# Attention and two MoE layers on one core: the first MoE's Strassen operands formed from PSUM during attention, and its second phase taken by weight tile with both token halves

## The chip, the cores and the metric

One core of one Trainium2 chip runs the whole program. The metric is the device time of one execution, in microseconds (us). TensorE is written PE, VectorE DVE, ScalarE ACT, GpSimd POOL; SP is the engine that issues the DMAs here. PE's granted clock is given as a share of its upper level: 1.00 is 2.4 GHz, 0.50 is 1.2 GHz.

## What is computed

```python
attn = attention(q, k, v)                    # 4 batches, 8 heads, 576 positions, window 128
x = attn.transpose(0, 2, 1, 3).reshape(2304, 512)
h = x @ w_in                                 # first MoE: 512 -> 2048
r = np.maximum(h, 0.0)
x = (r * r) @ w_out                          # 2048 -> 512
...
for e in range(8):                           # second MoE: gates P by Sinkhorn, then the experts
    out += P[:, e:e + 1] * (np.maximum(x @ w1[e], 0.0) @ w2[e])
```

## The kernel before

Every matrix product is done in three passes over operands that are cut into a high part (fp32r) and the rest: high by high, high by low, low by high (`mm3`, lines 126 to 128). A *split* is the making of such a pair: ACT copies the high part, then DVE or POOL subtracts it (`split_sb` from SBUF, lines 117 and 118; `split_ps` from PSUM, lines 121 and 122).

The 2304 tokens of the first MoE are five chunks: 256, then four of 512. Chunks 0 to 2 go through a plain loop over 16 blocks f of 128 hidden columns (`gemm1`, square of the ReLU on ACT line 914 and DVE line 917, `moe1_tail` two blocks later). The steps of attention are woven into that loop, and a scheduler orders the engines' queues there. PE's product `h` of a block has one PSUM bank, which comes free when DVE has read it at line 917.

Chunks 3 and 4 (the token halves, t = 0 and 1) go together through one level of Strassen with seven products. Attention leaves their raw tokens in `xr[0]` and `xr[1]` (ACT copy, line 436). After the last attention step, in the last four blocks of chunk 2 (`early_super`), seven token operands are formed: b11, b21 and b22 are quarters of the tokens, t1 to t4 are sums and differences of quarters (DVE, lines 810 to 816), and each of the seven is split. The sums of the weights (`super_sums`, lines 839 to 843) and their splits stand in the same queues. From there on the order is as written. The **super stage** then runs eight units u of seven products p each (`s_product`, `s_evict`); its results g, two blocks f by two token halves h per unit, go to DRAM (`d_g`).

The **second phase** multiplies g by `w_out`: 32 products j of 12 matmuls each, for the first half f = 0 to 15 and then for the second half f = 0 to 15 again. Every j loads its own weight tile w (512 KB) and its g tile (256 KB) by `b_load`, five products ahead and the first four during the last unit of the super stage; `b_split` cuts g two products ahead, with the subtraction on POOL. Beside it stand the preparations for the second MoE: `load_q` (tokens back from DRAM), `x_op` (its seven token operands, alternately on DVE and POOL), `sums_w1` and `split_w1`, and `keep`, which adds the two parts of a finished chunk on POOL and stores it.

Of the kernel before, what the change touches and what calls it, by code (L numbers as in the profile page):

```python
# [29 lines left out]
def attention_moe_moe2(  # L30
# [393 lines left out]

    def put_x(ps, hp, t0, n):
        o = 0
        while o < n:
# [186 lines left out]
    def keep(c, d):  # L614
        c0, n = chunk(c)
        if True:
            if c < NCH - 1:
# [183 lines left out]
    xr_stack = ExitStack()  # L801
    sps = ExitStack()
    sx, sr, ss, sslab = {}, {}, {}, {}
    NU = NF1 // 2

    def super_x(nm, eng):

        q = {(h, t): xr[t][:, 2 * h : 2 * h + 2] for h in range(2) for t in range(2)}
        if nm == "t1":
            nc.vector.tensor_sub(q[0, 0], q[0, 1], q[0, 0])  # L810
        elif nm == "t2":
            nc.vector.tensor_sub(q[0, 0], q[1, 1], q[0, 0])
        elif nm == "t3":
            nc.vector.tensor_sub(q[0, 1], q[1, 1], q[0, 1])
        elif nm == "t4":
            nc.vector.tensor_sub(q[1, 0], q[1, 0], q[0, 0])
        at = {"b11": (0, 0), "t1": (0, 0), "t2": (0, 0), "b21": (1, 0), "t4": (1, 0), "t3": (0, 1), "b22": (1, 1)}[nm]
        x = sx[nm] = sp.tile([P, 2, 2, CH], F32R, name=f"s{nm}")
        split_sb(q[at], x[:, 0], x[:, 1], (nc.vector, nc.gpsimd)[eng])
# [37 lines left out]
    def early_super(at):  # L857
        nonlocal sp
        if at == 0:
# [5 lines left out]
            super_x("b11", 0)  # L865
            super_x("b21", 1)
        elif at == 1:
            super_sums(0, False)
            super_sums(0, True)
            super_split(0, False)  # L870
            super_x("t1", 0)
        elif at == 2:
            super_split(0, True)
            super_x("t2", 0)
            super_x("t3", 1)
        else:
            super_raw(2)
            super_x("t4", 0)
            super_x("b22", 1)

    sp = None
    for c in range(PLAIN_CH):
        c0, n = chunk(c)
        if c == 1:
# [6 lines left out]
            xp2 = xr_stack.enter_context(tc.tile_pool(name="xp2", bufs=1))  # L891
            for i in range(PLAIN_CH, NCH):
                xr.append(xp2.tile([P, NK, CH], F32, name=f"xr{i}"))

# [47 lines left out]
    xr_stack.close()  # L942
    gp = m1.enter_context(tc.tile_pool(name="gp", bufs=1))
# [11 lines left out]
    def s_product(u, p):  # L955
# [3 lines left out]
        for k in range(2):  # L959
            mm3(ps, (w[:, k, 0], w[:, k, 1]), (x[:, 0, k], x[:, 1, k]), first and k == 0, k == 1, skip_group_check=True)  # L960
# [37 lines left out]
    btiles = {}  # L998
    bparts = {}

    def b_load(j):

        if j < 2 * NF1:
            h, f = divmod(j, NF1)
            w = mp.tile([P, 2, DM], F32R, name="w", tag=("b", "a")[j % 2], bufs=(4, 3)[j % 2])
            nc.sync.dma_start(raw(w), d_out[f])
            g = gp.tile([P, CH], F32, name="gq", tag="gq", bufs=6)
            nc.sync.dma_start(g, d_g[f // 2][:, f % 2, h])
            btiles[j] = w, g

    def b_split(j):

        if j < 2 * NF1:
            g = btiles[j][1]
            hl = [rp.tile([P, CH], F32R, name=nm, tag=tag, bufs=3) for nm, tag in (("gh", "rh"), ("gl", "rl"))]
            split_sb(g, *hl)
            bparts[j] = hl

    baccs = []

    def b_product(j, ds):
        h, f = divmod(j, NF1)
        (w, _), (gh, gl) = btiles[j], bparts[j]
# [9 lines left out]
    def finish_part(c, d, acc1):  # L1033
        split_ps(acc1, xh[c][:, d], xl[c][:, d])
        if c < NCH - 1:
# [8 lines left out]
    for u, p in slots:  # L1044
        if u == NU:
            b_product(0, (0, 1))
            b_load(4)
# [7 lines left out]
        if u < 3 and p in (2, 4, 6) and keeps and u:  # L1055
            keep(*keeps.pop(0))
# [13 lines left out]
    X_AT = {4: ("b11", 0), 5: ("b21", 1), 6: ("t1", 0), 7: ("t2", 1), 8: ("t3", 0), 9: ("t4", 1), 10: ("b22", 0)}  # L1070
# [591 lines left out]
```

## Time and profile before

| | us |
|---|---|
| median of 3 runs | 2074.07 (2073.59 to 2077.26) |
| the profiled execution, its own time | 2077.16 |
| its span, first to last instruction | 2075.5 |
| PE busy | 2022.5 (97% of the span) |
| DVE, ACT, POOL busy | 1430.1, 985.9, 1127.0 |
| early stage (from the last attention step to the end of chunk 2) | about 380 to 413 |
| super stage | about 413 to 506 |
| second phase | about 506 to 602 |

A timeline row gives start, length, engine, line, operation, tiles, and in brackets how long the engine stood idle before it and who released it. A row of waits gives who waited for whom, us in total, how many times, and the longest. A row of a group gives the count, then busy us and mean ns of one, then the idle time before it. PE's matmuls overlap: a record lasts longer than the distance to the next one.

### The profile page before, as it was taken

The numbers are of one execution on the slowest core, as the hardware profiler recorded it, in microseconds if no ns is written. First come the engines' busy times: TensorE is split into PE (matmuls) and PEld (weight loads), VectorE is DVE, ScalarE is ACT, GpSimd is POOL, SyncE is SP. The second block draws the span as 40 slices with busy tenths as digits, with TensorE's granted clock in tenths as the row PEclk, the third lists the DMA queues.
The fourth block names the chain that finished last, engine by engine and source line by source line (L and its number), as shares of the span: only waits on it lengthen the run. The fifth ranks groups of instructions, "written<-read, shape, count | busy, mean of one in ns | idle before, by whom it ended". The sixth has DMA issues, their size and how long they took to land.

```text
span 2075.5 us, 31718 instructions
## 1 busy us (share of the span) xinstructions
PE 2022.5 (97%) x10821; PEld 1844.5 (89%) x10821; DVE 1430.1 (69%) x2513; ACT 985.9 (48%) x1997; POOL 1127.0 (54%) x855
## 2 busy tenths in 40 slices
PE   7989999899999999999999999999999999999999
PEld 5767777677778899999998999999999999999999
DVE  7986766664336878777776667766776677677765
ACT  7666665354344554444444444444444443444443
POOL 4224344543678788878875445544554454455442
PEclk9999999999999999999999999999999999999999
DMA  7867777346968778888789877777786777777773
GB/s 212 276 205 245 225 223 200 112 148 214 324 236 294 291 293 315 325 306 317 290 301 351 273 260 254 257 260 257 245 285 221 263 259 257 254 257 241 266 259 109
DMA packets 298721, 528.08 MB, mean 254 GB/s; under 512 B 91312, under 2 KB 138048, under 8 KB 294464
## 3 DMA queue, kind: packets, MB, share of 16 engines
q1 hardware_dynamic: 298560, 526.04, 75.4%
q8 instruction: 87, 1.43, 0.3%
q14 instruction: 74, 0.61, 0.1%
HBM read 364.92 MB, written 161.03 MB: 253 GB/s over the span
## 4 chain that ended last, share of the span: by engine, by line
PE 80%; DVE 6%; DMA 3%; ACT 2%; POOL 2%; issue 2%; SPq 0%; ACTq 0%; POOLq 0%; DVEq 0%
PE y L127 11%; PE y L128 11%; PE y L126 11%; PE g L126 10%; PE g L128 10%; PE g L127 10%; PE acc L127 1%; PE acc L128 1%; PE s L126 1%; PE s L127 1%; PE s L128 1%; PE acc L126 1%; PE h L126 1%; PE h L128 1%; PE h L127 1%
## 5 line engine op out<-in xcount | busy, mean ns | idle before, releaser
L1470 POOL TENSOR_TENSOR rb<-R,rb 128x768 fp32r<-128x768 f32 x95 | 213.9, 2252 | 345.8 <-ACT rb L1465 317.4
L1506 DVE TENSOR_TENSOR a<-y,a 128x384 f32<-128x384 f32 x420 | 232.6, 554 | 193.1 <-PE y L128 192.7
L1470 POOL TENSOR_TENSOR rt<-R,rt 128x768 fp32r<-128x768 f32 x121 | 230.3, 1915 | 138.9 <-ACT rt L1465 60.0
L118 POOL TENSOR_TENSOR w2a<-r,w2a 128x1024 fp32r<-128x1024 f32 x64 | 154.0, 2407 | 67.3 <-ACT w2a L117 67.3
L126 PE MATMUL g<-xt,w1o 128*128 128x384 f32 x512 | 173.7, 339 | 2.3 <-ACT u L1184 1.0
L128 PE MATMUL g<-xt,w1o 128*128 128x384 f32 x512 | 172.6, 337 | 0.0
L127 PE MATMUL g<-xt,w1o 128*128 128x384 f32 x512 | 172.3, 337 | 0.0
L126 PE MATMUL y<-rt,w2o 128*128 128x384 f32 x496 | 168.1, 339 | 0.0
L127 PE MATMUL y<-rt,w2o 128*128 128x384 f32 x496 | 167.9, 339 | 0.0
L128 PE MATMUL y<-rt,w2o 128*128 128x384 f32 x496 | 167.4, 337 | 0.0
L1465 ACT ACTIVATE rt<-R 128x768 fp32r<-128x768 f32 x122 | 102.7, 842 | 134.9 <-DVE R L1451 84.1
L128 PE MATMUL y<-w2a,rl 128*128 128x512 f32 x384 | 150.1, 391 | 0.0
L127 PE MATMUL y<-w2a,rh 128*128 128x512 f32 x384 | 149.6, 390 | 0.2 <-POOL w2a L118 0.2
L126 PE MATMUL y<-w2a,rh 128*128 128x512 f32 x384 | 149.5, 389 | 0.0
L1446 DVE TENSOR_TENSOR R<-R,pb 128x768 f32<-128x768 f32 x128 | 138.4, 1082 | 5.5 <-ACT R L1572 3.9
L126 PE MATMUL y<-rb,w2o 128*128 128x384 f32 x408 | 138.3, 339 | 0.6 <-DVE a L1506 0.6
L127 PE MATMUL y<-rb,w2o 128*128 128x384 f32 x408 | 138.2, 339 | 0.0
L128 PE MATMUL y<-rb,w2o 128*128 128x384 f32 x408 | 137.6, 337 | 0.0
L126 PE MATMUL g<-xb,w1o 128*128 128x384 f32 x384 | 129.9, 338 | 0.0
L128 PE MATMUL g<-xb,w1o 128*128 128x384 f32 x384 | 129.5, 337 | 0.0
L127 PE MATMUL g<-xb,w1o 128*128 128x384 f32 x384 | 129.2, 337 | 0.0
L1572 ACT ACTIVATE R<-u 128x384 f32<-128x384 f32 x128 | 67.3, 526 | 127.6 <-DVE u L1192 86.4
(316 smaller groups left out, 5896.7 us busy)
## 6 DMA issues: line engine op xcount, KB each, us to landing
w1o<-d_w SPq DMA_DIRECT2D x448, 256.0 KB, 3.1
w2o<-d_w SPq DMA_DIRECT2D x218, 512.0 KB, 4.0
d_w<-w1a SPq DMA_DIRECT2D x32, 1792.0 KB, 11.5
d_w<-w2a SPq DMA_DIRECT2D x30, 1536.0 KB, 7.8
r<-in_moe_w_dram SPq DMA_DIRECT2D x64, 512.0 KB, 4.2
w<-d_out SPq DMA_DIRECT2D x32, 512.0 KB, 5.7
u<-in_moe_w_in_dram SPq DMA_DIRECT2D x16, 512.0 KB, 5.0
u<-in_moe_w_out_dram SPq DMA_DIRECT2D x16, 512.0 KB, 5.5
```

Of the source, the lines that this page charges most:

```text
L118: (eng or nc.gpsimd).tensor_sub(lo, src, raw(hi))
L126: nc.tensor.matmul(ps, lhsT=lh, rhs=rh, start=first, stop=False, **kw)
L127: nc.tensor.matmul(ps, lhsT=lh, rhs=rl, start=False, stop=False, **kw)
L128: nc.tensor.matmul(ps, lhsT=ll, rhs=rh, start=False, stop=last, **kw)
L1446: nc.vector.tensor_mul(r, r, pb[:, None, :].to_broadcast([P, 2, HALF]))
L1465: nc.scalar.activation(x[:, 0], R[m, f, h], AF.Copy)
L1470: eng.tensor_sub(x[:, 1], R[m, f, h], raw(x[:, 0]))
L1506: nc.vector.tensor_add(acc[dst][:, dt], ps[:, :HALF], acc[dst][:, dt])
L1572: nc.scalar.activation(R[m, f, h][:, pair], src, AF.Relu)
```

## The change

Three things are changed. **(1) Token operands.** As each piece of attention output for chunks 3 and 4 leaves PSUM, `put_super` forms operands from it at once. Pieces of the first half are split straight into b11 or b21, and copied to `xr[0]` as well. Pieces of the second half: for hp 0 and 1 (quarter b12) copied, and t1 = ps - b11 formed; for hp 2 and 3 (quarter b22) split, and t2 = ps - t1, t3 = ps - b12 (DVE) and t4 = b21 - t2 (POOL) formed. In `early_super` the splits of t1 to t4 remain, all on DVE. b11 and b21 have tiles of their own; b22, t1 and t2 lie in chunk 0's and chunk 1's token tiles, which are free by then. **(2) The second phase** goes by f with both halves in turn (`border`), so that each of the 16 weight tiles is loaded once; only the last two f are done half after half. All eight PSUM banks accumulate at once. **(3) Order of the preparations.** `b_load(0)` to `b_load(4)` stand in unit 6 instead of units 7 and 8, `b_split`'s subtraction and all of `x_op` go to DVE, chunk 2's `keep`s leave the super stage for j = 14 to 17, chunk 3's come at j = 29, its gate sums at j = 30, and g lands in the space of `xr`.

```diff
+    def put_super(ps, half, hp, at, w):
+        kh, k = divmod(hp, 2)
+        (r0, r1), ts = [[xr[t][:, x] for x in (k, 2 + k)] for t in range(2)], slice(at, at + w)
+        (b11, b21), (b12, b22) = r0, r1
+        if half == 0:
+            split_ps(ps, *[x[:, k, ts] for x in sx["b21" if kh else "b11"]])
+            nc.scalar.copy(r0[kh][:, ts], ps)
+        elif kh == 0:
+            nc.scalar.copy(b12[:, ts], ps)
+            nc.vector.tensor_sub(b11[:, ts], ps, b11[:, ts])
+        else:
+            split_ps(ps, *[x[:, k, ts] for x in sx["b22"]])
+            nc.vector.tensor_sub(b22[:, ts], ps, b11[:, ts])
+            nc.vector.tensor_sub(b12[:, ts], ps, b12[:, ts])
+            nc.gpsimd.tensor_sub(b21[:, ts], b21[:, ts], b22[:, ts])
...
-                nc.scalar.copy(xr[c - PLAIN_CH][:, hp, at : at + w], ps[:, o : o + w])
+                put_super(ps[:, o : o + w], c - PLAIN_CH, hp, at, w)
...
+    def super_x(nm):
+        if nm not in sx:
+            x = sp.tile([P, 2, 2, CH], F32R, name=f"s{nm}")
+            sx[nm] = x[:, 0], x[:, 1]
+        r = {"t1": xr[0][:, :2], "t4": xr[0][:, 2:], "t3": xr[1][:, :2], "t2": xr[1][:, 2:]}[nm]
+        split_sb(r, *sx[nm], nc.vector)
...
             super_raw(1)
-            super_x("b11", 0)
-            super_x("b21", 1)
+            super_x("t2")
+            super_sums(0, False)
         elif at == 1:
-            super_sums(0, False)
+            super_split(0, False)
             super_sums(0, True)
-            super_split(0, False)
-            super_x("t1", 0)
+            super_x("t1")
         elif at == 2:
             super_split(0, True)
-            super_x("t2", 0)
-            super_x("t3", 1)
+            super_x("t3")
         else:
             super_raw(2)
-            super_x("t4", 0)
-            super_x("b22", 1)
+            super_x("t4")
...
+    border = [(0, 0), (1, 0), (0, 1), (1, 1)] + [(f, h) for f in range(2, NF1 - 2) for h in range(2)]
+    border += [(f, h) for h in range(2) for f in (NF1 - 2, NF1 - 1)]
...
-        if j < 2 * NF1:
-            h, f = divmod(j, NF1)
-            w = mp.tile([P, 2, DM], F32R, name="w", tag=("b", "a")[j % 2], bufs=(4, 3)[j % 2])
-            nc.sync.dma_start(raw(w), d_out[f])
-            g = gp.tile([P, CH], F32, name="gq", tag="gq", bufs=6)
+        if j < len(border):
+            f, h = border[j]
+            if h == 0:
+                bw[f] = mp.tile([P, 2, DM], F32R, name="w", tag="ba"[f % 2], bufs=(4, 3)[f % 2])
+                nc.sync.dma_start(raw(bw[f]), d_out[f])
+            g = bg[j] = xr[j // NK % 2][:, j % NK]
             nc.sync.dma_start(g, d_g[f // 2][:, f % 2, h])
...
-            split_sb(g, *hl)
+            split_sb(bg.pop(j), *bparts[j], nc.vector)
...
-        if u < 3 and p in (2, 4, 6) and keeps and u:
-            keep(*keeps.pop(0))
...
-        elif u == NU - 1 and p < 4:
+        elif u == NU - 2 and p < 5:
             b_load(p)
-            if p > 1:
-                b_split(p - 2)
+        elif u == NU - 1 and p in (2, 3):
+            b_split(p - 2)
...
-    X_AT = {4: ("b11", 0), 5: ("b21", 1), 6: ("t1", 0), 7: ("t2", 1), 8: ("t3", 0), 9: ("t4", 1), 10: ("b22", 0)}
+    X_AT = {6: "b11", 7: "b21", 8: "t1", 9: "t2", 10: "t3", 11: "t4", 12: "b22"}
...
-        if j == 1:
+        if j == 2:
             load_q(0)
         elif j in X_AT:
-            nm, eng = X_AT[j]
-            x_op(nm, (nc.vector, nc.gpsimd)[eng])
-        elif j == 11:
+            x_op(X_AT[j], nc.vector)
+        elif j == 13:
             raw_w1(0)
             raw_w1(1)
...
-        if h == 1 and keeps and f > 4:
+        if keeps and 14 <= j < 20:
             keep(*keeps.pop(0))
```

What the change does to the queues is shown at three places. The first is DVE's queue of before behind the last score of attention, up to the second release of the bank of `h` (`sb` and `st` are split operands, `ss` the weights' sums, `r<-h` the read that frees PE's bank):

```order
L118 TENSOR_TENSOR sb_5147<-xr_2015,sb_5147 128x1024
L810 TENSOR_TENSOR xr_2015<-xr_2016,xr_2015 128x1024
L917 SCALAR_TENSOR_TENSOR r<-h_5157,r 128x512
L839 TENSOR_TENSOR ss<-sr 128x256
L843 TENSOR_TENSOR ss<-sr 128x256
L840 TENSOR_TENSOR ss<-ss,sr 128x256
L814 TENSOR_TENSOR xr_2016<-xr_2016 128x1024
L842 TENSOR_TENSOR ss<-sr,ss 128x256
L118 TENSOR_TENSOR st_5198<-xr_2015,st_5198 128x1024
L812 TENSOR_TENSOR xr_2015<-xr_2016,xr_2015 128x1024
L917 SCALAR_TENSOR_TENSOR r<-h_5205,r 128x512
```

The same stretch of DVE's queue now (the read that frees the bank is line 931 there; `xl_90` is the low part of b22, `xl_92` of t2):

```order
L122 TENSOR_TENSOR xl_90<-xo,xh_89 128x320
L440 TENSOR_TENSOR xr_2016<-xo,xr_2015 128x320
L441 TENSOR_TENSOR xr_2016<-xo,xr_2016 128x320
L118 TENSOR_TENSOR xl_92<-xr_2016,xl_92 128x1024
L118 TENSOR_TENSOR st_5279<-xr_2016,st_5279 128x1024
L850 TENSOR_TENSOR ss<-sr 128x256
L931 SCALAR_TENSOR_TENSOR r<-h_5202,r 128x512
L851 TENSOR_TENSOR ss<-ss,sr 128x256
L854 TENSOR_TENSOR ss<-sr 128x256
L853 TENSOR_TENSOR ss<-sr,ss 128x256
L118 TENSOR_TENSOR st_5322<-xr_2015,st_5322 128x1024
L931 SCALAR_TENSOR_TENSOR r<-h_5245,r 128x512
```

The four differences over 1024 columns (810 to 816; 816 stands behind these rows) are gone, and the split of t1 stands ahead of the last scores. On PE, three matmuls of `acc` have moved from behind to ahead of `h_5245`, so that 15 stand between the two `h`.

The second place is DVE's queue in the second phase. Before, it held only its share of the second MoE's token operands (`q` differences, `xb` and `xt` splits):

```order
L118 TENSOR_TENSOR xb_6207<-q,xb_6207 128x768
L712 TENSOR_TENSOR q<-q 128x768
L118 TENSOR_TENSOR xt_6254<-q,xt_6254 128x768
L714 TENSOR_TENSOR q<-q 128x768
L716 TENSOR_TENSOR q<-q 128x768
L118 TENSOR_TENSOR xt_6302<-q,xt_6302 128x768
L718 TENSOR_TENSOR q<-q 128x768
L118 TENSOR_TENSOR xb_6349<-q,xb_6349 128x768
```

Now the splits of g (`gl`) stand between them:

```order
L118 TENSOR_TENSOR xb_6256<-q,xb_6256 128x768
L118 TENSOR_TENSOR gl<-xr_2015,gh 128x512
L731 TENSOR_TENSOR q<-q 128x768
L118 TENSOR_TENSOR xt_6277<-q,xt_6277 128x768
L118 TENSOR_TENSOR gl<-xr_2015,gh 128x512
L733 TENSOR_TENSOR q<-q 128x768
L118 TENSOR_TENSOR xt_6300<-q,xt_6300 128x768
L118 TENSOR_TENSOR gl<-xr_2016,gh 128x512
```

POOL, which held 32 `gl` and three of the seven splits, holds none of them now.

The third place is SP's queue around the first loads of the second phase (`d_g<-gs` stores a result of the super stage, `w` and `gq` are loads). Before:

```order
L971 DMA d_g_279<-gs 128x512 x2
L1006 DMA w<-d_out_225 128x1024
L1008 DMA gq<-d_g_273 128x512
L971 DMA d_g_279<-gs 128x512 x2
L971 DMA d_g_280<-gs 128x512
L1006 DMA w<-d_out_226 128x1024
L1008 DMA gq<-d_g_273 128x512
L1006 DMA w<-d_out_227 128x1024
L1008 DMA gq<-d_g_274 128x512
```

Now:

```order
L983 DMA d_g_278<-gs 128x512 x2
L1020 DMA w<-d_out_225 128x1024
L1022 DMA xr_2015<-d_g_273 128x512
L983 DMA d_g_278<-gs 128x512 x2
L983 DMA d_g_279<-gs 128x512
L1020 DMA w<-d_out_226 128x1024
L1022 DMA xr_2015<-d_g_273 128x512 x3
L983 DMA d_g_279<-gs 128x512
L1020 DMA w<-d_out_227 128x1024
L1022 DMA xr_2016<-d_g_274 128x512
```

The first load stands one unit's stores earlier (behind `d_g_278`, unit 5, in place of `d_g_279`), and one w goes with two g.

## Rows read from the trace of the kernel before

**Rows 1.** The page's part 1, PE: busy us, share of the span, instructions.
```profile
PE 2022.5 (97%) x10821; PEld 1844.5 (89%) x10821; DVE 1430.1 (69%) x2513; ACT 985.9 (48%) x1997; POOL 1127.0 (54%) x855
```

**Rows 2.** Waits of PE from 380 to 600 us: total, times, longest.
```profile
PE h L126 <- DVE r L917: 7.2, 2, 6.1
PE acc L127 <- POOL gl L118: 3.2, 4, 0.9
PE s L126 <- ACT su L987: 3.0, 1, 3.0
PE s L127 <- POOL gl L118: 1.2, 1, 1.2
PE acc L126 <- ACT gh L117: 0.9, 1, 0.9
PE s L128 <- POOL sw L118: 0.7, 1, 0.7
```

**Rows 3.** PE's timeline: two matmuls in a row at full clock.
```profile
402.62 0.40 PE L128 MATMUL h<-xh,a 128*128 128x512 f32 x1
402.85 0.40 PE L126 MATMUL h<-xh,a 128*128 128x512 f32 x1
```

**Rows 4.** Windows after two stalls: busy us of each engine, PEclk, DMA share, GB/s.
```profile
399.00:403.00 4.00, 3.93 (x10) 3.14 (x11) 4.00 (x3) 2.08 (x3) 3.87 (x2) 0.55 0.05 18
...
501.00:505.00 4.00, 3.73 (x9) 2.97 (x10) 1.68 (x3) 1.41 (x3) 1.09 (x1) 0.57 0.70 262
```

**Rows 5.** DVE's timeline in the early stage.
```profile
381.99 1.23 DVE L118 TENSOR_TENSOR sb<-xr,sb 128x1024 fp32r<-128x1024 f32 x1 [3.59 <-DMA b<-d_out]
383.25 3.32 DVE L810 TENSOR_TENSOR xr<-xr,xr 128x1024 f32<-128x1024 f32 x1
...
387.09 2.02 DVE L839 TENSOR_TENSOR ss<-sr 128x256 f32<-128x256 f32 x1
...
393.58 0.41 DVE L842 TENSOR_TENSOR ss<-sr,ss 128x256 f32<-128x256 f32 x1
```

**Rows 6.** ACT's timeline: a split of 1024 columns, and the start of the second phase.
```profile
386.60 1.06 ACT L117 ACTIVATE st<-xr 128x1024 fp32r<-128x1024 f32 x1 [1.53 <-DVE xr L810]
...
500.11 0.63 ACT L117 ACTIVATE gh<-gq 128x512 fp32r<-128x512 f32 x1 [4.67 <-DMA gq<-d_g]
500.65 0.57 ACT L987 COPY su<-s 128x512 f32<-128x512 f32 x1
```

**Rows 7.** Groups by form in attention, 160 to 381 us, DVE and ACT.
```profile
L122 DVE TENSOR_TENSOR xl<-xo,xh 128x320 fp32r<-128x320 f32 x3 | 1.5, 487 | 0.4 <-ACT xh L121 0.4
L122 DVE TENSOR_TENSOR xl<-xo,xh 128x128 fp32r<-128x128 f32 x4 | 1.1, 286 | 0.0
L118 DVE TENSOR_TENSOR b<-b 128x512 fp32r<-128x512 f32 x13 | 9.1, 696 | 0.3 <-ACT b L117 0.2
L436 ACT COPY xr<-xo 128x320 f32<-128x320 f32 x8 | 3.4, 420 | 1.9 <-PE xo L420 1.7
```

**Rows 8.** Waits of PE from 160 to 380 us: the first and the last of six.
```profile
PE pt L400 <- ACT ks L292: 0.8, 1, 0.8
...
PE h L126 <- ACT a L117: 0.2, 1, 0.2
```

**Rows 9.** Windows: attention beside chunks 1 and 2, and two stretches around 127 us.
```profile
180.00:380.00 200.00, 196.53 (x1119) 151.86 (x1117) 137.27 (x489) 123.15 (x379) 82.35 (x152) 1.00 0.72 212
...
123.00:127.00 4.00, 2.23 (x10) 1.72 (x10) 3.82 (x14) 4.00 (x16) 0.00 (x0) 0.89 0.27 98
127.00:131.00 4.00, 4.00 (x16) 3.20 (x16) 2.41 (x7) 0.53 (x2) 1.22 (x2) 0.69 0.36 130
```

**Rows 10.** DVE's timeline in the second phase: 768 columns, POOL idle (first) and busy.
```profile
520.99 0.96 DVE L712 TENSOR_TENSOR q<-q 128x768 f32<-128x768 f32 x1
...
533.37 1.62 DVE L118 TENSOR_TENSOR xt<-q,xt 128x768 fp32r<-128x768 f32 x1 [0.91 <-ACT xt L117]
534.91 2.03 DVE L718 TENSOR_TENSOR q<-q 128x768 f32<-128x768 f32 x1
```

More of the change, by code (lines that the diff above doesn't have):

```diff
@@ L800, in attention_moe_moe2 @@
     qstack = []
-    xr_stack = ExitStack()
     sps = ExitStack()
-    sx, sr, ss, sslab = {}, {}, {}, {}
+    sr, ss, sslab = {}, {}, {}
     NU = NF1 // 2
[L806 to L819, printed above, removed]
+    def super_x(nm):
[4 more added lines that the diff above has]
+        split_sb(r, *sx[nm], nc.vector)
     def super_raw(u):
@@ L890, in attention_moe_moe2 @@
                     nc.gpsimd.memset(raw(x), 0.0)
-            xp2 = xr_stack.enter_context(tc.tile_pool(name="xp2", bufs=1))
+            xp2 = m1.enter_context(tc.tile_pool(name="xp2", bufs=1))
             for i in range(PLAIN_CH, NCH):
                 xr.append(xp2.tile([P, NK, CH], F32, name=f"xr{i}"))
+            for nm in ("b11", "b21"):
+                x = xp2.tile([P, 2, 2, CH], F32R, name=f"s{nm}")
+                sx[nm] = x[:, 0], x[:, 1]
+            sx["b22"] = [x[0].rearrange("p k c -> p (k c)").rearrange("p (k c) -> p k c", c=CH) for x in (xh, xl)]
+            for nm, x in (("t1", xh[1]), ("t2", xl[1])):
+                sx[nm] = x[:, :2], x[:, 2:]
         advance(needed(c0 + n))
@@ L959, in s_product @@
         for k in range(2):
-            mm3(ps, (w[:, k, 0], w[:, k, 1]), (x[:, 0, k], x[:, 1, k]), first and k == 0, k == 1, skip_group_check=True)
+            mm3(ps, (w[:, k, 0], w[:, k, 1]), (x[0][:, k], x[1][:, k]), first and k == 0, k == 1, skip_group_check=True)
     scount = [0]
@@ L996, in s_evict @@
             s_square(u, v2, 0, 1)
[L998 to L999 removed]
+    border = [(0, 0), (1, 0), (0, 1), (1, 1)] + [(f, h) for f in range(2, NF1 - 2) for h in range(2)]
+    border += [(f, h) for h in range(2) for f in (NF1 - 2, NF1 - 1)]
+    bw, bg, bparts, baccs = {}, {}, {}, []
     def b_load(j):
[L1003 to L1007 removed]
+        if j < len(border):
[4 more added lines that the diff above has]
+            g = bg[j] = xr[j // NK % 2][:, j % NK]
             nc.sync.dma_start(g, d_g[f // 2][:, f % 2, h])
[L1009 removed]
     def b_split(j):
[L1013 to L1019 removed]
+        if j < len(border):
+            bparts[j] = [rp.tile([P, CH], F32R, name=nm, tag=tag, bufs=3) for nm, tag in (("gh", "rh"), ("gl", "rl"))]
+            split_sb(bg.pop(j), *bparts[j], nc.vector)
     def b_product(j, ds):
[L1022 to L1023 removed]
+        f, h = border[j]
+        w, (gh, gl) = bw[f], bparts[j]
         for d in ds:
@@ L1069, in attention_moe_moe2 @@
     p3 = p3s.enter_context(tc.tile_pool(name="p3a", bufs=1, side="right"))
-    X_AT = {4: ("b11", 0), 5: ("b21", 1), 6: ("t1", 0), 7: ("t2", 1), 8: ("t3", 0), 9: ("t4", 1), 10: ("b22", 0)}
-    for j in range(2 * NF1):
-        h, f = divmod(j, NF1)
+    X_AT = {6: "b11", 7: "b21", 8: "t1", 9: "t2", 10: "t3", 11: "t4", 12: "b22"}
+    for j in range(len(border)):
         if j:
             b_product(j, range(NK))
-        btiles.pop(j)
         bparts.pop(j)
```

12 lines of the change are left out of this document (5 added, 7 removed).

## The prediction

> **What bounds the kernel now.** I read the page's busy times first: PE is busy for 2022.5 of 2075.5 us [rows 1], and the change leaves the number of matmuls as it is. So an edit can gain only where PE stands still or runs slowly, and it loses where it makes PE stand. The second view is therefore the list of PE's waits over the three stages that the change touches, 380 to 600 us [rows 2]: six lines with ten waits, 7.2 + 3.2 + 3.0 + 1.2 + 0.9 + 0.7 = 16.2 us (a seventh line of 0.2 is left out). The third is the clock behind the long ones. After PE stood 6.1 us for DVE, and again after the 3.0 us for ACT, the granted clock is 0.55 and 0.57 over 4 us [rows 4], so mostly at its lower level of 1.2 GHz; PE lost 3.93 x 0.45 = 1.8 us and 3.73 x 0.43 = 1.6 us there. A wait is counted from the modelled end of the matmul ahead, 0.40 us after its start, though the next could have started after 0.23 [rows 3]; so each of the ten waits cost 0.17 us more than its row, 1.7 us in all. Together 16.2 + 3.4 + 1.7 = 21.3 us of PE time lie open in these stages. By place: **early stage** 7.2 + 0.3 + 1.8 = 9.3; **super stage** 0.7 + 0.2 = 0.9; **second phase** (its seven waits for gl, su and gh) 8.3 + 1.2 + 1.6 = 11.1.
>
> Who makes PE wait? In the early stage it is the read of `h` at line 917, which stands in DVE's queue behind operand differences of 3.32 us and weight sums of 2.02 us apiece [rows 5]. At the start of the second phase it is a queue as well: ACT stands 4.67 us for a g tile to land, and the copy `su`, which PE needs for its bank, stands right behind that split [rows 6]. Later in the phase it is POOL's `gl`.
>
> **Early stage.** The change takes the four differences out of DVE's queue and leaves three splits and four sums of the weights there. I walk DVE's queue of the changed order from the last attention product; the first `h` starts right behind that, which I set to 0. ACT's copy to b22 (0.42) and DVE's three subtractions of 320 columns (0.49 each [rows 7]) are done at 2.0; t2's split can begin on ACT at 1.6 (1.06 [rows 6]), DVE follows at 2.7 with 1.23 [rows 5], and t3's 1.23 ends at 5.2. One weight sum takes 0.41 or, as at 387, 2.02 [rows 5]; the read of `h` itself, in PSUM, I estimate at 0.7 from the 0.70 of 512 columns [rows 7]. So the bank is free at 6.3 or 7.9. PE wants it after 12 + 15 matmuls at 0.23, at 6.2: a stall of 0.1 to 1.7. For the next read three sums (1.2 to 6.1), t4's split (1.23) and the read must fit into 12 + 9 matmuls, 4.8: they need 3.1 if no sum is held, 5.0 with one held, 8.0 with all. So the residue lies between 0.1 and, with the first stall, 1.7 + 3.2 = 4.9. I take 1.0, near the lower end, since POOL's 1024-column splits that stood beside DVE at 383 have left the stage. No gap is then near the 6.1 us that the clock fell after. Gain 9.3 - 1.0 = 8.3; bounds 9.2 and, with the clock fallen again, 2.6.
>
> **Attention, which gets that work.** Per head pair, the first half's three pieces (128, 320, 64 columns) get a DVE subtraction and an ACT copy each; the second half's two (192, 320) get one DVE subtraction for hp 0 and 1, three for hp 2 and 3. On DVE: 4 x 0.29 and (4 + 8) x 0.49 [rows 7], with 64 and 192 columns estimated at 0.22 and 0.35 from these two, 4 x 0.22 and 8 x 0.35: 10.7 us. On ACT: 4 x 0.42 [rows 7] and, scaled by width, some 0.25 and 0.2 for the others: 3.5 us. On POOL four subtractions, of which only t4 depends. Between 180 and 380 us DVE is busy for 137 of 200 us, ACT for 123, PE for 197 [rows 9]: the cover is 63 us of idle DVE, and PE's waits there are only six, 2.9 us in all [rows 8]. But the work comes in bursts, ahead of score reductions in DVE's queue, and holds one of three attention banks longer. Bounds: from 1.5 below nothing (the scheduler sets a new order here, which could as well take half of the 2.9 away) to 14.2 if all of it stands in PE's way. I take 1.5, half of today's waits again, because PE at 98% is what DVE's queue waits for in that stretch, and not the reverse.
>
> **Super stage.** The 0.7 us wait for a weight split on POOL came where chunk 2's `keep`s stood in POOL's queue; they are moved to j = 14 to 17, where POOL is nearly empty. Gain 0.9; the five loads that are now issued in unit 6 find free buffers and stand behind stores of finished results, so no store waits for them long. At nothing.
>
> **Second phase.** All first loads are asked for seven products sooner, 42 matmuls or 9.6 us, which is more than the 4.67 that ACT stood; so `su` no longer waits behind g. Sixteen loads of 512 KB are gone. `gl` moves from POOL to DVE, at 0.70 [rows 7] a step. What may come late is DVE during t1 to t4 (j = 8 to 11): a difference 0.96 [rows 10], ACT's 0.80 (three quarters of 1.06), a subtraction of 0.92 (three quarters of 1.23 [rows 5]), and `gl` 0.70 make 3.4 us per product, and PE takes 12 x 0.23 = 2.7. Four times 0.7 is a lag of 2.6. A split may start when the product three ahead of its own has freed the tile, and is needed two products later, 5.5 us; less its own 0.63 + 0.70 that leaves 4.1 us of slack. The lag is covered. Product j = 2 writes the banks of the super stage's last results: add, ReLU and square, 0.70 + 0.57 + 0.70 [rows 6, 7], are read out some 2 us after the last of its products, and 18 matmuls, 4.1 us, lie between. I leave 0.5 for the phase's start: gain 11.1 - 0.5 = 10.6, bounds 11.1 and 4.0 (next part). The gate sums of chunk 3 and its `keep`s move as whole groups to the phase's end: the same matmuls, and POOL has the length of two products for four additions; at nothing.
>
> In rows 10 the same difference over 768 columns takes 0.96 with POOL idle and 2.03 with POOL splitting. This is what the Trainium skill states in "SBUF — State Buffer", section "Who interferes with whom": a DVE instruction with both inputs in SBUF and a GpSimd instruction that reads SBUF exclude each other for a whole instruction, and one with an input in PSUM does not take part. By that rule the operands of j = 6 to 12 run at the short durations, as POOL has nothing there, and nothing formed from PSUM in attention is held; were the slow rows due to something else, the phase would come out as in the third case below.
>
> **The sum.** 8.3 + 0.9 + 10.6 - 1.5 = 18.3 us. Against the profiled execution, 2077.16, this is 2058.9; that execution lies 3.1 above the median of the runs, and I hold the gain against the median: 2074.07 - 18.3 = **2055.8**.
>
> **The rivals.**
> *Attention pays.* All 14.2 us stand in PE's way: 21.3 - 1.5 - 14.2 = 5.6 gained, **2068.5**. For it: bursts of three subtractions ahead of the scores. Against: PE's few waits there [rows 8].
> *The early stage stays late.* DVE's sums are held by POOL all through, 4.9 us remain and the clock falls again (1.8): 18.3 - 3.9 - 1.8 = 12.6, **2061.5**. That is the case in which the change doesn't do what it says.
> *DVE becomes the bound of the second phase.* At the long durations [rows 10] a product needs 2.03 + 0.80 + 1.62 + 0.70 = 5.15, four times 2.4 over PE's pace, 9.6; less 4.1 of slack 5.5 us of stall, and the clock falls (1.6): 18.3 - 5.5 + 0.5 - 1.6 = 11.7, **2062.4**. Against it: POOL is empty there.
> *Slower: the clock falls in attention.* At 123 to 127 us PE worked for 2.23 of 4 us, and then ran at 0.69 [rows 9]: 1.8 + 1.2 = 3.0 us for one such gap. If the longer hold of an attention bank opens one in each head pair's batch that the change touches (16), it decides against the gain of 19.8 from the seventh on; at ten it costs 30, **2084**. Against: at 98% busy nothing like it is near now.
>
> **How the numbers follow.** Chances: forecast 0.70, attention pays 0.10, early stage 0.07, DVE's bound 0.08, clock 0.05. Low end: all 21.3 gone and 1.5 gained in attention, 2051.3. High end: 2066, past the second and third rival and half of the way that attention's bounds reach; left out are attention at its full price, the clock, and some 0.05 below. 0.2% of this time, about what a measurement can tell from no change, is 4.1 us: faster means below 2069.9. Forecast, early stage, DVE's bound and half of "attention pays" are well clear of it, 0.90; half of that case, with something else late as well, lands within, 0.05; slower 0.05.
>
> **What would show it.** Right: PE's waits for the read of `h` after the last attention step fall from 7.2 to 2 us or less, with no clock below 1.00 there; `su` no longer waits behind a g split, and PE's waits in the second phase nearly vanish; DVE's 768-column differences take about 1 us. Wrong: PE's waits between 160 and 380 us rise well above 2.9 us or its clock falls there; or PE waits for `gl` on DVE at j = 9 to 13; or the stretch after 602 us, which I hold to be untouched, changes its length by microseconds.

## The result and the profile after

The changed kernel takes **2055.86 us** (median of 4 runs, 2055.26 to 2057.16), the kernel before on the same chip 2075.33 (2073.59 to 2077.26). The ratio is 0.9907, with a 95% interval of 0.989 to 0.9924: 19.5 us faster. The profiled execution after took 2057.16 us, its span is 2055.4, against 2077.16 and 2075.5 before, so the two spans differ by 20.1.

The page's part 1 of the kernel after (busy us, share of the span, instructions of each engine) answers to [rows 1]. PE has the same 10821 matmuls and is busy 98% of the span. DVE has 59 instructions more, POOL 34 fewer:

```profile
PE 2017.4 (98%) x10821; PEld 1843.2 (90%) x10821; DVE 1440.3 (70%) x2572; ACT 986.0 (48%) x2006; POOL 1069.4 (52%) x821
```

PE's waits from 380 to 600 us after the change (total, times, longest). Of the 16.2 us of [rows 2] 1.2 are left, in these two lines (the others, 0.6, 0.6 and 0.2, belong to the second MoE's `g` and `y`, behind the stages in question):

```profile
PE s L126 <- ACT su L999: 0.9, 1, 0.9
...
PE h L126 <- DVE r L931: 0.3, 1, 0.3
```

To see where the 20.1 us of span went, four marks are enough: the first `h` behind the last attention step, the first product of the super stage, the last product of the second phase, the end. PE's timeline of the kernel before (start, length, line, tiles):

```profile
380.35 0.50 PE L126 MATMUL h<-xh,a 128*128 128x512 f32 x1
...
414.43 0.39 PE L126 MATMUL s<-sb,sw 128*128 128x512 f32 x1
...
600.07 0.40 PE L128 MATMUL s<-gh,w 128*128 128x512 f32 x1
```

And of the kernel after:

```profile
381.27 0.50 PE L126 MATMUL h<-xh,a 128*128 128x512 f32 x1
...
406.46 0.39 PE L126 MATMUL s<-sb,sw 128*128 128x512 f32 x1
...
579.70 0.39 PE L128 MATMUL s<-gh,w 128*128 128x512 f32 x1
```

| stage | before | after | measured | predicted |
|---|---|---|---|---|
| up to the first `h` behind attention | 380.35 | 381.27 | +0.9 (0.4 of it before 142 us, ahead of the change) | +1.5 |
| early stage | 34.1 | 25.2 | -8.9 | -8.3 |
| super stage and second phase | 185.6 | 173.2 | -12.4 | -0.9 - 10.6 = -11.5 |
| the rest | 1475.4 | 1475.7 | +0.3 | 0 |

The third line can be taken apart by windows of the two stages (length, busy us of PE, PEld, DVE, ACT, POOL with counts, PEclk, DMA share, GB/s). Before:

```profile
414.43:506.00 91.57, 86.87 (x369) 68.45 (x368) 52.74 (x88) 46.13 (x77) 37.45 (x20) 0.98 0.49 163
506.00:600.07 94.07, 89.58 (x390) 71.45 (x389) 20.02 (x21) 30.79 (x50) 57.68 (x41) 1.00 0.82 278
```

After:

```profile
406.46:492.30 85.84, 84.96 (x367) 67.28 (x366) 50.94 (x89) 46.02 (x77) 31.06 (x15) 1.00 0.46 153
492.30:579.70 87.40, 87.40 (x386) 71.91 (x386) 39.09 (x54) 30.62 (x49) 14.29 (x11) 1.00 0.63 223
```

PE stood for 4.70 + 4.49 = 9.2 us before and stands for 0.88 + 0.00 after: 8.3 of the 12.4. The other 4.1 are busy time: 1.6 for the clock [rows 4], 0.17 for each of the eight waits that are gone (nine before, one after), 1.4, and some 0.35, an estimate, for four small matmuls of the gate sums that have moved behind the phase (390 records, then 386). That leaves some 0.8 us for which these rows give no cause.

### The profile page after: what moved, and what is told of

The parts are those of the page before. It is cut to its first block, busy times and chain, and to the rows that moved or that the text cites. A ratio compares the mean times of both kernels' runs of the same rounds, so it can differ in the third digit from the quotient of the medians.

```text
span 2055.4 us, 31706 instructions
## 1 busy us (share of the span) xinstructions
PE 2017.4 (98%) x10821; PEld 1843.2 (90%) x10821; DVE 1440.3 (70%) x2572; ACT 986.0 (48%) x2006; POOL 1069.4 (52%) x821
## 4 chain that ended last, share of the span: by engine, by line
PE 83%; DVE 6%; ACT 2%; DMA 2%; issue 1%; POOL 1%; SPq 0%; ACTq 0%; DVEq 0%; POOLq 0%
PE y L127 11%; PE y L126 11%; PE y L128 11%; PE g L126 11%; PE g L127 10%; PE g L128 10%; PE s L126 2%; PE s L128 2%; PE s L127 2%; PE acc L127 2%; PE acc L128 2%; PE acc L126 2%; PE h L126 1%; PE h L128 1%; PE h L127 1%
## 5 line engine op out<-in xcount | busy, mean ns | idle before, releaser
L127 PE MATMUL g<-xt,w1o 128*128 128x384 f32 x512 | 172.3, 337 | 0.0
```

What stands on the lines that cost most here:

```text
L127: nc.tensor.matmul(ps, lhsT=lh, rhs=rl, start=False, stop=False, **kw)
```

## The experiments

The first question was whether the two halves of the change, operands formed early and the new second phase, bring what their stages show. The second was why `su` still waits, which the prediction said it would not.

Beside the median, each run below can be read by the marks of its one profile. They are sharper than the medians for these stages, because executions of one kernel already differ by some 3 us before anything that the change touches: the first `h` near 140 us starts at 141.92 in the kernel after and at 138.75 when the same kernel ran once more (x0). The super stage and the second phase together:

| run | first product of the super stage | last product of the second phase | us between |
|---|---|---|---|
| before | 414.43 | 600.07 | 185.6 |
| x2, old second phase | 404.84 | 590.75 | 185.9 |
| x9, POOL's token splits on DVE | 410.55 | 596.53 | 186.0 |
| x3, loads sooner alone | 413.79 | 599.27 | 185.5 |
| x11, x3 with own tiles | 414.58 | 594.28 | 179.7 |
| x5, w loaded 32 times | 402.89 | 582.64 | 179.7 |
| x4, `gl` on POOL | 405.55 | 582.21 | 176.7 |
| x10, x5 with a fourth buffer | 402.98 | 578.12 | 175.1 |
| after | 406.46 | 579.70 | 173.2 |
| x0, after once more | 403.42 | 576.48 | 173.1 |
| x1, operands late | 413.73 | 586.76 | 173.0 |
| x6, subtractions twice | 409.37 | 582.20 | 172.8 |
| x8, first product whole | 403.51 | 575.80 | 172.3 |
| x12, x8 with a fourth buffer | 405.36 | 577.63 | 172.3 |

The four runs with the second phase of the kernel after unchanged (after, x0, x1, x6) lie within 0.4 us.

**Operands formed late, new second phase (x1).** Chunks 3 and 4 leave attention by the ACT copy as before, and all operands are formed in `early_super`.

```diff
-                put_super(ps[:, o : o + w], c - PLAIN_CH, hp, at, w)
+                nc.scalar.copy(xr[c - PLAIN_CH][:, hp, at : at + w], ps[:, o : o + w])
...
-            super_x("t2")
-            super_sums(0, False)
+            super_x("b11", 0)
+            super_x("b21", 1)
```

> The new second phase alone: attention leaves raw tokens as before, and all seven operands are formed and split in the early stage. Theory (the early stage's stall is the queue of differences and sums ahead of the read of h): PE's wait for that read comes back to about 7 us in two waits, the granted clock falls behind the long one, and of the gain of 19.5 us some 9 are lost: 10 to 11 us faster than before, about 2065. Rival (the second phase would take the stall up anyway, the parts do not add): 15 us or more stay.

Measured: 2062.35 us, ratio 0.9935 (0.9919 to 0.9952), 13.5 us faster than before, some 3 more than expected. Its line of waits and two rows of DVE's queue in the early stage say why:

```profile
PE h L126 <- DVE r L944: 4.6, 2, 3.4
```

```profile
381.70 1.22 DVE L830 TENSOR_TENSOR xr<-xr,xr 128x1024 f32<-128x1024 f32 x1 [2.56 <-ACT xr L455]
...
383.98 3.44 DVE L834 TENSOR_TENSOR xr<-xr 128x1024 f32<-128x1024 f32 x1
```

The scheduler set the same pieces in another order than in the kernel before. Two of the first three differences ran at 1.22 us, where [rows 5] show 3.32 for the first, and PE waited 4.6 us, not 7.2. From the last `xo` to the super stage x1 takes 32.8 us where before took 34.2. So 1.4 of the 13.5 belong to that order, and the new phase is worth some 12.1, which agrees with the 12.4 of the table. (8.3 of x2 and 13.5 add up to 2.3 more than the whole; that order is 1.4 of it.)

**Operands formed early, old second phase (x2).** The second phase, its loads and the `keep`s are those of before.

```diff
-    border = [(0, 0), (1, 0), (0, 1), (1, 1)] + [(f, h) for f in range(2, NF1 - 2) for h in range(2)]
-    border += [(f, h) for h in range(2) for f in (NF1 - 2, NF1 - 1)]
+    border = [(f, h) for h in range(2) for f in range(NF1)]
```

> The operands from PSUM alone: second phase, its loads, splits, keeps and preparations in the old order and on the old engines. Theory: the early stage stays short (waits for the read of h 0.3 us, clock 1.00), attention costs 0.5 to 1.5 us, and the old waits of the second phase (su 3.0, gl 4 to 5 us, clock at half for 3.4 us) come back: 8 to 9 us faster than before, about 2067. Rival (attention pays for the early stage): less than 5 us faster, with PE's waits from 160 to 380 us above 5 us.

Measured: 2067.6 us, 0.9961 (0.9946 to 0.9976), 8.3 us faster, as expected. Its waits show the early stage as in the kernel after and the second phase as in [rows 2]:

```profile
PE s L126 <- ACT su L999: 2.9, 1, 2.9
PE acc L127 <- POOL gl L118: 2.9, 4, 0.9
...
PE h L126 <- DVE r L931: 0.3, 1, 0.3
```

**POOL's three token splits on DVE (x9).** The prediction laid DVE's long rows of [rows 5] to POOL's splits beside them. In the kernel before, these go to DVE. That gives DVE's queue more work.

```diff
-            super_x("b21", 1)
+            super_x("b21", 0)
...
-            super_x("t3", 1)
+            super_x("t3", 0)
...
-            super_x("b22", 1)
+            super_x("b22", 0)
```

> The kernel before with one edit: the three token splits of the early stage that POOL makes (b21, t3, b22) go to DVE. Theory A (DVE's pieces were long because POOL's splits held them): DVE gets three more pieces of 1.2 us, but its differences shorten from 3.3 to about 1.2 us and its sums from 2.0 towards 0.4; PE's wait for the read of h falls from 7.2 to 2 to 5 us, 2 to 6 us faster than before. Theory B (the number of pieces in DVE's queue decides): the wait grows by up to 3.7 us, to about 10, and the kernel is 2 to 4 us slower than before.

Measured: 2072.31 us, 0.9981 (0.9972 to 0.999), 3.6 us faster than before with three more splits in the queue that PE waits for, as theory A said. PE's wait for `h` fell from 7.2 to 4.3. DVE's timeline:

```profile
383.23 1.22 DVE L810 TENSOR_TENSOR xr<-xr,xr 128x1024 f32<-128x1024 f32 x1
...
384.96 1.67 DVE L839 TENSOR_TENSOR ss<-sr 128x256 f32<-128x256 f32 x1
```

The difference of line 810 took 3.32 us in [rows 5] and takes 1.22 here, the three others 1.21. The sum of line 839 stays long, at 1.67, and POOL's split of a weight (384.50 to 386.36) still runs beside it. The long rows were time in which POOL worked on SBUF, not a cost of the operation.

**DVE's subtractions of `put_super` twice (x6).** All of them are issued a second time, into a spare tile or with the same result, so DVE gets the work of the change in attention twice over: 28 pieces and 10.7 us more (the 36 in the expectation is a miscount).

```diff
             split_ps(ps, *[x[:, k, ts] for x in sx["b22"]])
+            nc.vector.tensor_sub(lo, ps, raw(hi))
+            nc.vector.tensor_sub(spare[0][:, :w], ps, b11[:, ts])
+            nc.vector.tensor_sub(spare[0][:, :w], ps, b12[:, ts])
```

> The changed kernel with every DVE subtraction of the operands' forming done twice (36 pieces of 64 to 320 columns become 64 or so, 10.7 us more on DVE; the doubles go to the same place or to a spare tile). Theory (idle DVE covers it): at most 1.5 us slower than the changed kernel, PE's waits from 160 to 380 us below 6 us. Rival (attention pays piece by piece): about 10 us slower.

Measured: 2060.78 us, 0.993 (0.9917 to 0.9942), 5.3 us slower than the kernel after in the same comparison (2055.5). This is neither the 1.5 nor the 10, and the place is not the expected one. By PE's matmuls attention itself grew by 1.4 us (240.7 against 239.3 in x0, from the first `h` near 140 us to the last `xo`), the early stage by 3.1. Its waits, and a window behind the stall:

```profile
PE h L126 <- DVE r L939: 2.5, 1, 2.5
```

```profile
394.00:398.00 4.00, 3.98 (x10) 3.12 (x11) 0.00 (x0) 0.63 (x1) 2.81 (x2) 0.57 0.48 149
```

Three more pieces of 320 columns stand behind the last attention product, and the scheduler put the splits behind the sums. PE stood 2.5 us and its clock fell to the lower level. So attention's cover is real: 10.7 us of DVE work more cost 1.4. The margin behind it is small: a few pieces more at the stage's end bring a stall back.

**Only the loads asked for sooner (x3).** In the kernel before, `b_load(0)` to `b_load(4)` move to unit 6, as in the change, and nothing else.

```diff
-        elif u == NU - 1 and p < 4:
+        elif u == NU - 2 and p < 5:
             b_load(p)
-            if p > 1:
-                b_split(p - 2)
+        elif u == NU - 1 and p in (2, 3):
+            b_split(p - 2)
```

> The kernel before with one edit: its first five loads of the second phase stand in unit 6 of the super stage, the splits where they were. Theory (the phase's start is held by the moment of the request): ACT no longer stands 4.67 us for g, PE's wait for su falls from 3.0 to 1 or less, the wait for the first gl goes and the clock stays up: 4 to 6 us faster than before, about 2070; the waits for gl at 523 to 535 and 585 us stay. Rival (the bytes asked for hold it): the g tiles land as late as before and less than 2 us are gained.

Measured: 2073.72 us, 0.9988 (0.9979 to 0.9997), 2.2 us faster, half of what was expected, and in its profile `su` waits for 3.0 us as before. The profiled execution is the slowest of the ten (2070.17 to 2077.15). It gained nothing in these stages. PE stood for 7.9 us in place of 9.2, but behind the same wait for `su` the clock stayed low for longer: 0.58 over the 8 us from 499, against 0.79 over the 8 us from 501 in the kernel before. Why other executions were faster is not shown. ACT's timeline there, and the transfer issued at 489.99 (count, KB, us from issue to landing):

```profile
493.33 0.65 ACT L117 ACTIVATE gh<-gq 128x512 fp32r<-128x512 f32 x1
498.73 0.63 ACT L117 ACTIVATE gh<-gq 128x512 fp32r<-128x512 f32 x1 [4.75 <-DMA gq<-d_g]
499.26 0.57 ACT L987 COPY su<-s 128x512 f32<-128x512 f32 x1
```

```profile
d_g<-gs SPq DMA_DIRECT2D x1, 256.0 KB, 8.7
```

The row names a load, but by the issues and landings that g tile had landed at 489.39, nine us before. What landed at 489.99 + 8.66 = 498.65, just ahead of the 498.73, is a *store* of the super stage. The second split's high part `gh` and every other result `gs` on its way to `d_g` share one tag with three buffers (lines 969 and 1015 of the kernel before). The split could not write until that store had read its buffer, and the store was queued behind loads. Asking sooner took away one wait and put another in its place.

**The kernel after, with w loaded for each product (x5).** The order of the products and the tiles are the new ones, but the weight tile is fetched 32 times again.

```diff
-            if h == 0:
-                bw[f] = mp.tile([P, 2, DM], F32R, name="w", tag="ba"[f % 2], bufs=(4, 3)[f % 2])
-                nc.sync.dma_start(raw(bw[f]), d_out[f])
+            bw[j] = mp.tile([P, 2, DM], F32R, name="w", tag="ba"[j % 2], bufs=(4, 3)[j % 2])
+            nc.sync.dma_start(raw(bw[j]), d_out[f])
```

> The changed kernel, but every product of the second phase loads its weight tile anew (32 loads of 512 KB in place of 16), in the new order, five products ahead. Theory (the bytes were not what held the phase; the moment of the request and POOL's splits were): PE waits for no DMA there, and the time is within 1 us of the changed kernel. Rival (sharing the weight tile brought the gain): waits for w or g come back, 3 us or more slower than the changed kernel.

Measured: 2062.6 us, 0.9937 (0.9925 to 0.995), 7.1 us slower than the kernel after beside it. The bytes that the prediction had left without a price are a third of the gain. The profiled execution is the fastest of the five (2059.4 to 2064.16). By the marks the two stages take 6.7 us more than in x0: 4.3 of it are PE's longer waits (4.9 in all, against 0.6) and some 1.5 the clock behind the first (0.79 from 488 to 496 us). The two longer waits, ACT's second split and the store issued at 478.44:

```profile
PE s L126 <- ACT su L999: 4.0, 1, 4.0
...
PE s L126 <- ACT gh L117: 0.7, 1, 0.7
```

```profile
487.93 0.63 ACT L117 ACTIVATE gh<-xr 128x512 fp32r<-128x512 f32 x1 [5.42 <-DMA d_g<-gs]
```

```profile
d_g<-gs SPq DMA_DIRECT2D x1, 256.0 KB, 9.4
```

Here the row names the store itself. In the kernel after the same split waits for the same store, only less long. Its chain of waits (start, us, what) is read downwards: store, split, copy, matmul:

```profile
485.81 2.43 DMA d_g<-gs
...
488.33 0.63 ACT gh L117
488.96 0.48 ACT su L999
...
489.49 0.50 PE s L126
```

The store that holds this split's tile was issued at 481.66 and landed 6.57 us later, at 488.23. (The chain's first row starts at 485.81 because it names a later store, some of whose updates came at the same moment; that one landed as a whole at 489.49, after the split had begun.) Stores with no loads ahead of them land in 2.0 (two of the kernel after, issued from 491.5 to 494 us):

```profile
d_g<-gs SPq DMA_DIRECT2D x2, 256.0 KB, 2.0
```

**x5 with a fourth buffer (x10).** If the bytes matter only through that store, a fourth buffer for the shared tag should bring x5's loss back with all 32 loads in place.

```diff
-            gh = rp.tile([P, CH], F32R, name="gh", tag="rh", bufs=3)
+            gh = rp.tile([P, CH], F32R, name="gh", tag="rh", bufs=4)
...
-        g = raw(rp.tile([P, CH], F32R, name="gs", tag=("rh", "rl")[i], bufs=3))
+        g = raw(rp.tile([P, CH], F32R, name="gs", tag=("rh", "rl")[i], bufs=(4, 3)[i]))
```

> The changed kernel with its weight tiles loaded twice, as in the run on that, and a fourth buffer for the tiles that hold a square on its way to DRAM or the high part of a split. Theory (the second split on ACT waited for a store, which frees its tile and had queued behind the loads for 9.4 us): PE's wait for su falls from 4.0 to 1 us or less, the clock stays up, and some 5 of the 7 us against the changed kernel come back, about 2057. Rival (the extra bytes hold the g tiles themselves): the wait for su stays above 3 us, no gain.

Measured: 2055.53 us (2055.35 to 2055.64), 0.9902 (0.9887 to 0.9916): by the medians all 7 us are back. By the marks it is the "some 5" of the expectation: 4.6 us less than x5, and 2 more than the kernel after. Medians of four and five runs, in different comparisons, can't tell the two readings apart. The stores are as late as in x5 (two issued from 474 to 480 us took 9.4), but no line of `su` is left in PE's waits, and ACT cuts the first two g tiles without a pause:

```profile
481.97 1.16 ACT L117 ACTIVATE gh<-xr 128x512 fp32r<-128x512 f32 x2
```

What PE waits for instead is DVE's addition right behind that copy, and later three splits of g:

```profile
PE s L126 <- DVE s L1001: 0.7, 1, 0.7
...
PE acc L127 <- DVE gl L118: 0.6, 2, 0.3
PE s L127 <- DVE gl L118: 0.3, 1, 0.3
```

So that store was most of what the 16 extra loads cost, but not all of it.

**x3 with tiles of their own for the first two high parts (x11).**

```diff
-            hl = [rp.tile([P, CH], F32R, name=nm, tag=tag, bufs=3) for nm, tag in (("gh", "rh"), ("gl", "rl"))]
+            hl = [gp.tile([P, CH], F32R, name="gh0", tag="gh0", bufs=2)] if j < 2 else [rp.tile([P, CH], F32R, name="gh", tag="rh", bufs=3)]
+            hl.append(rp.tile([P, CH], F32R, name="gl", tag="rl", bufs=3))
```

> The kernel before with its first five loads in unit 6, as in the run on that, and tiles of their own for the high parts of the first two splits. Theory (as above: there the store took 8.7 us): PE's wait for su falls from 3.0 to 1 us or less and the clock does not fall there; 4 to 6 us faster than before, about 2070. Rival: the wait only moves on, to the landing of g, and 2 us or less are gained.

Measured: 2069.91 us, 0.9969 (0.9958 to 0.9981), 6.0 us faster than before and 3.8 more than x3 gave; by the marks 5.9 and 5.8. The wait for the copy of line 987 is gone, the clock is 1.00 from 494 to 504 us, and ACT cuts the first two tiles in one go (a wait of 0.2 for another copy, of line 982, is left, and the kernel before has it too):

```profile
494.06 1.16 ACT L117 ACTIVATE gh<-gq 128x512 fp32r<-128x512 f32 x2
```

So in the kernel before, too, the start of the phase needs both: loads asked for sooner and a buffer that no store holds. x11 and x10 start from kernels that differ in many ways, but in each a buffer free of stores takes the wait for `su` away, and that shows the mechanism. Own buffers without the sooner loads were not tried.

**The first product in one piece (x8), and with the fourth buffer (x12).** The kernel after runs the first half of product 0 between two products of unit 7 and the other half behind the last. x8 puts all of it between them, so PE has six matmuls more before it wants the bank that `su` frees; x12 adds the fourth buffer.

```diff
-            b_product(0, (0, 1))
+            b_product(0, range(NK))
             continue
...
-    b_product(0, (2, 3))
```

> The changed kernel with the second phase's first product whole (12 matmuls, not 6) between units' products 4 and 5 of the last unit, in place of half there and half at the end. Theory: the 0.9 us that PE still waits for su is covered by six more matmuls, 0.9 to 1.1 us faster than the changed kernel. Rival: the banks of the last results are read out too late for product j = 2, which has 12 matmuls less half of them to wait, and the same time is lost there: no change.

> The changed kernel with its first product whole and the fourth buffer together. Theory: no wait for su is left by the whole product alone, so the fourth buffer adds nothing that can be measured: 0 to 1 us faster than with the whole product alone, about 2054. Rival (the store's landing holds more than that wait): 2 us or more faster.

Measured: x8 2054.24 us (2053.46 to 2055.11), ratio 0.9901 (0.9886 to 0.9916); x12 2054.64 (2054.26 to 2055.17), 0.9898 (0.9883 to 0.9912). The kernel after once more beside x8 (**x0**): 2055.5 (2053.33 to 2057.1), 0.9905 (0.9891 to 0.9918), with 0.6 us of wait for `su`. In x8 ACT waits 2.32 us for the store as before, but PE does not, and no line of `su` is left in either. The two have the lowest medians, by about 1 us, which is no more than the runs of one kernel differ among themselves. By the marks both are 0.8 to 1.0 us shorter than the kernel after and x0, as was expected of x8, and the fourth buffer adds nothing, as was expected of x12; that rests on one profile of each.

> The changed kernel again, on the chip and beside the runs of before that the other kernels of this call are held against: 18 to 21 us faster than before.

**`gl` back on POOL (x4).** The kernel after with the splits of g subtracted by POOL.

```diff
-            split_sb(bg.pop(j), *bparts[j], nc.vector)
+            split_sb(bg.pop(j), *bparts[j])
```

> The changed kernel, but the 32 splits of g have their subtraction on POOL as before; the seven splits of token operands stay on DVE. Theory (POOL and DVE hold each other): a gl takes 1.3 to 2.0 us on POOL and DVE's pieces of 768 columns at j = 6 to 12 lengthen from about 1.0 to 1.6 to 2.0 us; PE waits 2 to 6 us in all for gl there, and the kernel is that much slower than the changed one. Rival (the sooner loads and the halved bytes did it all): no waits for gl, within 1 us of the changed kernel.

Measured: 2058.47 us (2058.08 to 2059.49), 0.9914 (0.9897 to 0.993), 2.6 us slower than the kernel after by the medians, though the intervals of the two ratios overlap. The marks are clearer: 3.4 to 3.6 us more in the two stages, within the 2 to 6 expected. Its waits, and DVE's and POOL's rows during the token operands:

```profile
PE s L127 <- POOL gl L118: 1.8, 2, 0.9
...
PE acc L127 <- POOL gl L118: 0.5, 1, 0.5
```

```profile
512.70 0.95 DVE L731 TENSOR_TENSOR q<-q 128x768 f32<-128x768 f32 x1
...
515.66 2.02 DVE L733 TENSOR_TENSOR q<-q 128x768 f32<-128x768 f32 x1
...
515.57 1.29 POOL L118 TENSOR_TENSOR gl<-xr,gh 128x512 fp32r<-128x512 f32 x1 [0.76 <-ACT gh L117]
```

The difference that starts 0.09 us after a `gl` of POOL takes 2.02, the one with POOL idle at its start 0.95. So DVE and POOL hold each other there, as expected, but PE does not wait there. Its three waits come later, at 543.23, 546.78 and 579.77, each for a `gl` that stood in POOL's queue behind a `keep`:

```profile
540.66 1.29 POOL L641 TENSOR_TENSOR x<-xh,xl 128x512 f32<-128x512 f32 x1 [2.64 <-DMA d_x<-x]
541.91 1.27 POOL L118 TENSOR_TENSOR gl<-xr,gh 128x512 fp32r<-128x512 f32 x1
```

The size came as expected, by another cause than the one named: the order in POOL's queue. The move of `gl` to DVE is worth its place, and without it the two stages still gain 9.0 of their 12.4.

## Why the prediction held, and which step did not

The forecast was 2055.8 and the time is 2055.9, in the middle of its range. That the two agree to 0.1 is luck: the gain was forecast at 18.3 us and is 19.5, and the kernel before took 2075.33 beside the result, 1.3 more than the 2074.07 that the forecast starts from. The two differences cancel. The steps one by one:

**What bounds the kernel** held: 15 of the 16.2 us of waits are gone, the two falls of the clock with them, and the rest of the program kept its length. In attention the waits went from 2.9 us [rows 8] to 3.5 (eight waits in six lines before; the prediction's "only six" counts the lines). This line grew most, from 0.4:

```profile
PE pt L400 <- DVE s L383: 1.8, 2, 1.2
```

It is hardly the mechanism of the first rival, scores that come late behind the bursts on DVE. The 1.2, at 287.92, is the wait that cost 0.8 in the kernel before (287.58, put down to ACT in [rows 8]), and DVE's queue holds no new piece in the 3 us ahead of it. Only the other, 0.6 at 216.29 where 0.4 stood before, has a new piece of 0.29 ahead of the score row. From the first `h` near 140 us to the one behind attention the change costs 0.5 us (0.7 in x0) where 1.5 was taken and up to 14.2 allowed. The clock there is 1.00 all through, so the slower rival had no case, and x6 shows that twice the work would have cost 1.4 more.

**Early stage**: 8.9 gained for 8.3, 0.3 of wait for the 1.0 taken. DVE's timeline after, to be read against the walk in the prediction:

```profile
385.04 1.22 DVE L118 TENSOR_TENSOR st<-xr,st 128x1024 fp32r<-128x1024 f32 x1
386.18 0.42 DVE L850 TENSOR_TENSOR ss<-sr 128x256 f32<-128x256 f32 x1
386.52 0.69 DVE L931 SCALAR_TENSOR_TENSOR r<-h,r 128x512 f32<-128x512 f32 x1
387.12 1.47 DVE L851 TENSOR_TENSOR ss<-ss,sr 128x256 f32<-128x256 f32 x1
388.51 1.51 DVE L854 TENSOR_TENSOR ss<-sr 128x256 f32<-128x256 f32 x1
```

The bank is free at 387.21, 5.9 us after the first `h` at 381.27, where the walk gave 6.3 or 7.9 and PE wants it at 6.2. The 0.3 that PE waits belongs to the next read. The first sum ran free (0.42), the next two were held part of the time (1.47, 1.51), beside POOL's weight splits. x9 shows the reason: without POOL's splits the long rows shrink. (In the walk's second part one held sum gives 2.84 + 1.23 + 0.70 = 4.8 us, not 5.0; the sum does not use it.)

**DVE as the bound of the second phase** did not come: the pieces of 768 columns take 0.95 or 0.96 there, and PE waits for no `gl`. Two rows of DVE and one of POOL in the kernel after show both cases for a `gl`, without and with a `keep` of POOL beside it:

```profile
523.68 0.69 DVE L118 TENSOR_TENSOR gl<-xr,gh 128x512 fp32r<-128x512 f32 x1
...
527.03 1.78 DVE L118 TENSOR_TENSOR gl<-xr,gh 128x512 fp32r<-128x512 f32 x1
...
526.77 1.48 POOL L641 TENSOR_TENSOR x<-xh,xl 128x512 f32<-128x512 f32 x1 [44.00 <-DMA d_x<-x]
```

The prediction named a rule of the Trainium skill here, "SBUF — State Buffer", section "Who interferes with whom". These rows, x4 and x9 agree with it: the three splits moved off POOL alone took DVE's difference from 3.32 to 1.22.

**The step that failed** is what the sooner loads do to the stores. Of the super stage the prediction says that these loads "stand behind stores of finished results, so no store waits for them long", and puts that at nothing; it looked at the stores ahead of the loads and not at those behind them. Stores issued from 474 to 485 us in the kernel before landed in 2.3 to 2.4 us; in the kernel after those behind the loads took up to 6.57. With that the conclusion on the second phase falls too: the loads are asked for 9.6 us sooner, more than the 4.67 that ACT stood [rows 6], "so `su` no longer waits behind g". Neither of the first two splits waits for g now, but `su` still waits, for 0.9 us, and 0.6 in x0, behind a split that waits for a store. The row of before named the load of g, and that was true there: the tile was asked for at 495.12 and landed 4.88 us later, at 500.01. But it was the last of two conditions. The other was the buffer of the high part, which a store held until 495.48, and a store that is issued behind more loads comes later. x3 has the sooner loads alone and gains 2.2 where the same reasoning gave 4 to 6; x11 adds the buffers and gains 6.0. Two things kept the error small. The halved loads of w, which the prediction mentions and gives no price, shorten that queue (x5: 7.1 us without them), and the 0.5 us it left "for the phase's start" is nearly the size of what stayed. That the term of 10.6 came out nearly right, with a piece missing on each side, is luck as well.

**The super stage**, up to the first matmul that reads w (495.57 before, 487.08 after), went from 81.1 to 80.6 us, 0.5 gained for the 0.9 forecast; the wait for the weight split on POOL (0.7) is gone, as forecast.

What stays open: some 0.8 us of the gain in the super stage and the second phase without a row, some 0.9 of x5's loss by the marks, and about half of the 2 us by which x10 is slower than the kernel after by the marks. The third part of the change, the order of the preparations, was not tried by itself, except for the first loads (x3) and `gl` (x4).

## What to carry to other kernels

A wait that the profile puts down to a late load ends at the last of several conditions: before asking for the load sooner, look who holds the tile that the waiting instruction writes, and when that holder's store lands behind the loads you are about to put ahead of it. Bytes taken out of a queue can be worth more than their share of bandwidth, and a single buffer more may give back most of them (x10). And before an engine's long rows are taken as its cost, see whether they are long only beside another engine's work on the same memory.

## What the runs showed of the hardware

- **Stores behind loads.** A store of 256 KB to DRAM landed 2.0 us after its issue with no load ahead of it, 6.6 in the kernel after, 8.7 in x3 and 9.4 in x5, where loads of w and g had been issued on the same queue in the microseconds before. In the three late cases the split that was to write its SBUF tile started 0.1 us behind that landing.
- **POOL pays too.** Where DVE and POOL met, it was not DVE alone that lost: the `gl` of POOL in x4 took 1.29 us in the row above and 1.96 when it started 0.15 us behind the start of DVE's difference at 512.70, which ran at its short 0.95:

```profile
512.85 1.96 POOL L118 TENSOR_TENSOR gl<-xr,gh 128x512 fp32r<-128x512 f32 x1 [0.89 <-ACT gh L117]
```

- **The clock behind short stalls.** After x6's wait of 2.5 us the granted clock was 0.57 over the next 4 us, so mostly at 1.2 GHz, though PE was busy for 3.98 of them; after the 0.9 us of the kernel after it was 1.00 (484 to 494 us). In the kernel after, with 0.3 us of wait in that stage, it was 1.00 throughout.
